# The first 60 steps of a layer, ordered by a list scheduler in the kernel instead of by hand-set pacing

## The chip, the cores and the metric

The kernel runs on one core of one Trainium2 chip. The metric is device time in microseconds (us) of one execution; the time of a kernel is the median of several runs.

## The reference

Three stages follow one another on 4 x 576 = 2304 tokens of width 512. Attention with 8 heads of 64: k and v are first averaged over groups of 8 positions (72 remain), then softmax(q k' / 8) v'. A gated layer with hidden width 1536:

```
gate = 1.0 / (1.0 + np.exp(-(x @ w_gate)))
val = x @ w_val
return (gate * val @ w_out).astype(np.float32)
```

Last, a mixture of 8 experts of width 1024 whose gates are normalised by 8 rounds of row and column division. The gated layer's weights are float64.

## The kernel before, in words

**Tiling.** The tokens are cut into 6 blocks of 384 (`NBLK`), and the 1536 hidden columns into 12 pieces of 128 (`NF1`). A step (j, f) of the gated layer takes block j and piece f: a gate product G and a value product V (12 matmuls each, L286: 4 pieces of the inner dimension times 3 passes over high and low halves), g = sigmoid(G) * V (sigmoid L1026 on ScalarE, product L1030 on VectorE), the high half of g (L1031, ScalarE) and its low half (L1034, VectorE), and an output product X of 12 matmuls (L644, `x2_step`) which sums into four PSUM banks. The table `steps1` sets the order of the 72 steps: blocks 0, 1 and 2 are interleaved over the first 36, then blocks 3, 4 and 5 follow one after the other. Steps 0 to 59 are those of blocks 0 to 4.

**Attention of a block** must end ahead of the block's first step: loads of k, v and q on SP's queue, sums over k (`pool_k`, VectorE) and over v (`pe_pool_v` on TensorE for two batches, `pool_v` on VectorE for the others), six groups of scores (`scores`), row maxima and subtraction (`less_max`), exponential (`softmax`), division (`invert`, `divide`), six groups of transposes (`turn_a`), three groups of `values`, and the split of the result into a high (L495) and a low half (L496), `xs`.

**Weights.** Each 128 x 512 piece of a weight (a chunk, 36 in all, named g, v or o) comes as float64 words into one of 4 tiles `wide`, is scaled (L197 on ScalarE, or L206 on VectorE for the first two), narrowed to float32 by five VectorE operations (L167, L168, L171, L172, L175) into one of 4 tiles `made`, and split into a high (L252) and a low half (L254) in one of 11 tiles `wa`. Its first user splits it; it is stored to DRAM (`words`), and blocks 2 to 5 load it from there. So VectorE prepares 12 chunks for the first six steps, and 24 more by step 29.

**What sets the order.** Each engine works off its own list, in the order in which the program issues. Attention is a generator (`attention`) cut by `yield` into pieces; the loop over the steps calls `slot` three times a step, and a running credit lets it take a piece there. `slot` also issues a whole chunk's narrowing when the running sums `until["dve"]` and `until["pe"]` (fixed costs added up as instructions are issued) leave room. `need` issues whatever a product still lacks, at once. Attention of block 0 and the first two score groups of block 1 are written out ahead of the first step; X of step n is issued behind G and V of step n + 1.

Of the kernel before, what the change touches and what calls it, by code (L numbers as in the profile page):

```python
# [9 lines left out]
F32 = mybir.dt.float32  # L10
# [10 lines left out]
def attention_moe_moe_kernel(  # L21
# [119 lines left out]
    n_wload = [0]  # L141
    n_split = [0]
    pools = {}
    later = []
    n_tick = [0]


    until = {"dve": 0, "pe": 0}
    loaded, scaled = [], []

    def load_wide():
        i = n_wload[0]
        if i >= n_wide:
            return
        n_wload[0] += 1
        t = xring.tile([128, KT * TB], U32, tag="fx", name="wide", bufs=NWIDE)
        nc.sync.dma_start(out=t[:, 0:1024], in_=WSRC["gvo"[i % 3]][i // 3].bitcast(U32))
        loaded.append((i, t[:, 0:1024].rearrange("p (c w) -> p c w", w=2)))

    def narrow_ops(i, raw):  # L160

        low, high = raw[:, :, 0], raw[:, :, 1]
        y = pools["at"].tile([128, 512], F32, tag="made", name="made", bufs=NMADE)
        x = y.bitcast(U32)
        v = nc.vector
        return y, [
            lambda: v.tensor_scalar(out=x, in0=high, scalar1=0x80000000, scalar2=None, op0=ALU.bitwise_and),  # L167
            lambda: v.scalar_tensor_tensor(  # L168
                out=x, in0=high, scalar=3, in1=x, op0=ALU.logical_shift_left, op1=ALU.bitwise_or
            ),  # L170
            lambda: v.tensor_scalar(out=high, in0=x, scalar1=0xFF800000, scalar2=None, op0=ALU.bitwise_and),  # L171
            lambda: v.scalar_tensor_tensor(  # L172
                out=f32(low), in0=low, scalar=2.0**-52, in1=f32(high), op0=ALU.mult, op1=ALU.mult
            ),
            lambda: v.tensor_tensor(out=y, in0=f32(low), in1=y, op=ALU.add),  # L175
        ]

    owing = [0]

    def narrow_tick():  # L180

        n_tick[0] += 1
        while owing[0]:
            owing[0] -= 1
            load_wide()
        if scaled and scaled[0][0] < n_used[0] + NMADE:
            i, raw = scaled.pop(0)
            y, ops = narrow_ops(i, raw)
            for op in ops:
                op()  # L190
            until["dve"] += 2950
            made[i] = y, n_tick[0]
            owing[0] += 1
        if loaded and not scaled:
            i, raw = loaded.pop(0)
            high = raw[:, :, 1]
            nc.scalar.activation(out=f32(high), in_=f32(high), func=AF.Copy, scale=2.0**-112)  # L197
            scaled.append((i, raw))

    def scaled_ops():  # L200

        i, raw = loaded.pop(0)
        high = f32(raw[:, :, 1])
        y, ops = narrow_ops(i, raw)
        return [
            lambda: nc.vector.tensor_scalar(  # L206
                out=high, in0=high, scalar1=2.0**-112, scalar2=None, op0=ALU.mult
            )
        ] + ops + [lambda: made.update({i: (y, -1)})]

    made = {}
    n_used = [0]
# [7 lines left out]
    stores = []  # L220
    n_kept = [0]

    def keep(k):

        while len(stores) > k:
            m, w = stores.pop(0)
            nc.sync.dma_start(out=words[m], in_=f32(w).rearrange("p s c -> p (s c)"))
            n_kept[0] += 1

    def split_chunk():  # L230

        i = n_split[0]
        if i >= len(chunks):
            return False
        m, first = source(i)
        if first:
            if m not in made or (loaded and n_tick[0] == made[m][1]):
                return False
# [1284 lines left out]
```

## Time and profile before

| what | us |
|---|---|
| median of 3 runs (2117.67 to 2124.04) | 2123.05 |
| the profiled execution's own time | 2118.32 |
| its span, first to last instruction | 2116.6 |
| TensorE busy (96%) | 2041.9 |
| VectorE busy (59%) | 1257.3 |
| ScalarE busy (36%) | 771.5 |

The profile is of one execution. An engine is busy while it executes; the time between is idle, and the profile names what ended each wait. PE is TensorE's matmuls, PEld its weight loads, DVE VectorE, ACT ScalarE, POOL GpSimd, SP the queue that issues the transfers. Busy times of matmuls overlap a little, as they are pipelined. The granted clock is 1.00 where TensorE runs at 2.4 GHz and 0.50 at 1.2 GHz; a stretch with both has a value between.

### The profile page before, as it was taken

How to read it: one execution, taken by the hardware profiler on the slowest of the kernel's cores; microseconds unless marked ns; L12 is line 12 of the kernel's file. 1: busy time of each engine (PE TensorE's matmuls, PEld its weight loads, DVE VectorE, ACT ScalarE, POOL GpSimd, SP SyncE). 2: the span in 40 equal slices, each digit the busy share in tenths (PEclk: the TensorE clock that was granted, in tenths of full speed). 3: DMA queues.
4: the chain of work that ended last, by engine and by line, in shares of the span. 5: the costliest groups of instructions: out<-in, count | busy, mean ns of one | idle time of the engine just before them, and what ended most of it. 6: DMA issues, size and time to landing. Idle time of an engine off the chain costs nothing.

```text
span 2116.6 us, 33177 instructions
## 1 busy us (share of the span) xinstructions
PE 2041.9 (96%) x12721; PEld 1943.6 (92%) x12721; DVE 1257.3 (59%) x2276; ACT 771.5 (36%) x1517; POOL 711.8 (34%) x645
## 2 busy tenths in 40 slices
PE   7778999999999999999999999999999999999998
PEld 5678989999997988998888999999999999999998
DVE  6677873523226877666665656565565556565655
ACT  4423322222224444344343444444443333333332
POOL 0000001010214474544542656655664222222322
PEclk9889999999999999999999999999999999999999
DMA  6447666776976686766768887788779876767674
GB/s 222 151 177 242 225 223 235 250 261 215 348 297 239 253 309 246 269 250 243 262 231 342 308 279 277 278 291 284 280 275 342 291 264 237 260 232 261 236 255 157
DMA packets 171853, 544.82 MB, mean 257 GB/s; under 512 B 15984, under 2 KB 65136, under 8 KB 155312
## 3 DMA queue, kind: packets, MB, share of 16 engines
q1 hardware_dynamic: 171216, 541.14, 71.8%
q8 instruction: 100, 1.64, 0.3%
q0 software_dynamic: 480, 1.57, 0.2%
q14 instruction: 57, 0.47, 0.1%
HBM read 376.72 MB, written 165.94 MB: 256 GB/s over the span
## 4 chain that ended last, share of the span: by engine, by line
PE 86%; DVE 7%; DMA 3%; ACT 3%; issue 1%; POOL 0%; SPq 0%; ACTq 0%; DVEq 0%; POOLq 0%
PE big L1263 22%; PE at L1111 18%; PE gv L1111 14%; PE big L1142 12%; PE gv L286 11%; PE big L644 5%; PE at L397 1%; PE at L485 1%; DMA wide<-in_moe_w_out_dram 1%; DVE wa L254 1%; DVE wide L172 1%; DVE made L168 1%; ACT wa L252 1%; DVE made L175 1%; DMA b<-w2d 1%
## 5 line engine op out<-in xcount | busy, mean ns | idle before, releaser
L286 PE MATMUL gv<-xs,wa 128*128 128x384 f32 x1728 | 334.1, 346 | 16.7 <-DVE g L1030 11.6
L1202 POOL TENSOR_TENSOR s<-hs,s 128x384 fp32r<-128x384 f32 x192 | 194.9, 1016 | 412.1 <-ACT s L1205 261.2
L286 PEld LDWEIGHTS gv<-xs,wa 128*128 128x128 f32 x1728 | 306.8, 193 | 24.9 <-DVE g L1030 14.1
L1142 PE MATMUL big<-w2hl,h 128*128 128x512 f32 x1152 | 297.0, 394 | 0.0
L1245 DVE SCALAR_TENSOR_TENSOR acc<-big,prob,acc 128x256 f32<-128x256 f32 (+1 forms) x462 | 254.7, 585 | 46.1 <-PE big L1263 46.1
L1142 PEld LDWEIGHTS big<-w2hl,h 128*128 128x128 f32 x1152 | 213.9, 188 | 34.3
L1111 PE MATMUL at<-xf,fs 128*128 128x384 f32 x1152 | 236.3, 340 | 3.7 <-ACT c L1314 2.7
L1111 PE MATMUL gv<-xf,fs 128*128 128x384 f32 x1152 | 233.4, 337 | 0.0
L1111 PE MATMUL at<-xf,fa 128*128 128x384 f32 x1152 | 228.0, 337 | 5.1 <-DVE gv L1332 1.8
L1111 PEld LDWEIGHTS at<-xf,fa 128*128 128x128 f32 x1152 | 198.5, 188 | 11.9 <-DVE gv L1332 2.5
L1111 PEld LDWEIGHTS at<-xf,fs 128*128 128x128 f32 x1152 | 196.8, 188 | 8.8 <-ACT c L1314 3.0
L1111 PEld LDWEIGHTS gv<-xf,fs 128*128 128x128 f32 x1152 | 198.2, 189 | 5.4 <-issue 0.2
L644 PE MATMUL big<-h,wa 128*128 128x384 f32 x864 | 166.0, 341 | 5.8 <-ACT wa L252 5.3
L1263 PE MATMUL big<-t,s 128*128 128x256 f32 x1152 | 162.7, 282 | 0.8 <-DVE acc L1245 0.8
L678 POOL TENSOR_TENSOR fx<-x,fx 128x768 fp32r<-128x768 f32 x10 | 18.4, 1836 | 426.8 <-ACT fx L677 426.8
L644 PEld LDWEIGHTS big<-h,wa 128*128 128x128 f32 x864 | 153.5, 192 | 7.8 <-ACT wa L252 6.2
L1263 PE MATMUL big<-b,a 128*128 128x256 f32 x1152 | 158.7, 283 | 2.0 <-DVE a L1192 1.9
L1263 PEld LDWEIGHTS big<-t,s 128*128 128x128 f32 x1152 | 157.1, 189 | 1.0 <-DVE acc L1245 1.0
L1263 PEld LDWEIGHTS big<-b,a 128*128 128x128 f32 x1152 | 153.5, 190 | 2.7 <-DVE a L1192 2.6
L1327 DVE TENSOR_TENSOR gv<-gv,c 128x384 f32<-128x384 f32 x64 | 36.2, 566 | 196.4 <-PE gv L1111 189.8
L1171 DVE SCALAR_TENSOR_TENSOR acc<-big,prob,acc 128x512 f32<-128x512 f32 x144 | 107.5, 747 | 70.8 <-PE big L1142 68.9
L1205 ACT ACTIVATE s<-hs 128x384 fp32r<-128x384 f32 x192 | 100.6, 524 | 110.9 <-DVE hs L1198 110.9
(184 smaller groups left out, 3067.2 us busy)
## 6 DMA issues: line engine op xcount, KB each, us to landing
wa<-words SPq DMA_DIRECT2D x144, 512.0 KB, 4.6
fs<-fsd SPq DMA_DIRECT2D x64, 1024.0 KB, 8.0
fa<-fad SPq DMA_DIRECT2D x64, 768.0 KB, 6.4
b<-w2d SPq DMA_DIRECT2D x192, 256.0 KB, 5.0
raw<-in_moe_w_dram SPq DMA_DIRECT2D x64, 512.0 KB, 7.6
fsd<-fs SPq DMA_DIRECT2D x32, 1024.0 KB, 6.2
w2d<-w2hl SPq DMA_DIRECT2D x32, 1024.0 KB, 3.9
fad<-fa SPq DMA_DIRECT2D x32, 768.0 KB, 5.8
```

The lines of the kernel that those rows point to most:

```text
L168: lambda: v.scalar_tensor_tensor(out=x, in0=high, scalar=3, in1=x, op0=ALU.logical_shift_left, op1=ALU.bitwise_or),
L172: lambda: v.scalar_tensor_tensor(out=f32(low), in0=low, scalar=2.0**-52, in1=f32(high), op0=ALU.mult, op1=ALU.mult),
L286: nc.tensor.matmul(out=out_, lhsT=a[s], rhs=b[m], start=(i == 0), stop=(i == n - 1))
L644: nc.tensor.matmul(out=x2p[d][:, :TB], lhsT=w[s][:, d * 128 : (d + 1) * 128], rhs=gs[j, f][m], start=(first and i == 0), stop=(last and i ...
L1111: nc.tensor.matmul(out=pt[:, :TB], lhsT=w[:, s, i, k], rhs=t[:, o, k], start=(start and m == 0), stop=(m == 5), skip_group_check=True,)
L1142: nc.tensor.matmul(out=py, lhsT=h[:, s, cs], rhs=w2hl[n][:, o, fh], start=(m == 0), stop=(m == 5))
L1171: nc.vector.scalar_tensor_tensor(out=acc[t], in0=py, scalar=pr, in1=acc[t], op0=ALU.mult, op1=ALU.add)
L1202: nc.gpsimd.tensor_tensor(out=t[:, 1], in0=x, in1=f32(t[:, 0]), op=ALU.subtract)
L1205: nc.scalar.activation(out=t[:, 0], in_=x, func=AF.Copy)
L1245: nc.vector.scalar_tensor_tensor(out=o, in0=src, scalar=pr, in1=o, op0=ALU.mult, op1=ALU.add)
L1263: nc.tensor.matmul(out=o, lhsT=hp[n0 + k, h][:, s, i * 128 : (i + 1) * 128], rhs=pieces2[n0, w][:, k, b], start=(first and m == 0), stop=( ...
L1327: nc.vector.tensor_tensor(out=vc, in0=vc, in1=c2, op=ALU.add)
```

## The change

The generator, `slot`, `need`, the credit and the running sums go. Each piece of the work of steps 0 to 59 becomes a task with an engine, a duration in us, the tasks that it needs, the places in tile rings that it takes and gives back (`room`, `frees`), a key (the step by which it is due, with an offset) and at times an earliest step. `Plan.run` keeps a clock for each engine. At each moment a free engine takes the task with the lowest key among those whose inputs have ended and whose room is free; taking it issues its instructions. So the lists of the engines follow the reckoned times. SP's transfers end at the reckoned end of all earlier ones plus size over 0.34 MB/us, plus 1.9 us.

Other differences: block 1's softmax is done like block 0's (one exponential with a sum for each head, straight from the scores; `j < DIRECT`); the narrowing of a chunk is two tasks (`narrow_high`, `narrow_low`) and its split two more; the division inverts for each 128 rows by itself; all of the attention of blocks 0 and 1 is due ahead of the first step. Steps 60 to 71 are issued by the loop as before.

```
+    class Plan:
+        LAG = 0.1
+        RATE = 0.34
+        REACH = 1.9
...
+        def run(self):
...
+            while left:
...
+                for e, l in queues.items():
+                    if free[e] > now:
+                        continue
+                    for t in l:
+                        if all(d.end is not None and d.end + self.LAG <= now for d in t.deps) and self.fits(t):
+                            break
+                    else:
+                        continue
+                    l.remove(t)
...
+                    t.emit()
+                    free[e] = now + t.dur
+                    t.end = now + t.dur
+                    if t.size:
+                        self.link = max(self.link, now + t.dur) + t.size / self.RATE
+                        t.end = self.link + self.REACH
...
+        def chunk(i):
...
+            n -= 0.9
+            w = add(n - 5, "SP", 0.4, lambda: load_wide(m), room=[("wide", 1)], size=0.524)
+            eng, dur = ("DVE", 0.42) if m < 2 else ("ACT", 0.68)
+            s = add(n - 0.3, eng, dur, lambda: scale_wide(m, eng), [w])
+            a = add(n, "DVE", 1.13, lambda: narrow_high(m), [s], room=[("made", 1)])
+            b = add(n, "DVE", 1.82, lambda: narrow_low(m), [a], frees=[("wide", 1)])
+            c = add(
+                n, "ACT", 0.63, lambda: split_high(i), [b], room=[("wa", 1)], cond=turn_of(i), after=took
+            )
+            d = add(n, "DVE", 0.69, lambda: split_low(m), [c], frees=[("made", 1)])
...
+        V_LATE = 0.3
+        DIRECT = 2
+        LEAD = {0: 30.0, 1: 28.0, 2: 6.0, 3: 10.0, 4: 10.0, 5: 10.0}
...
+        def attend(j):
+            n = float(at_step[j, 0] if j else 0)
+            lead = LEAD[j]
+            lo = n - lead
+            if j == 1:
+                lo, lead = -24.0, 24.0 + n - 0.5
...
+                    m = add(
+                        key, "DVE", 0.93 if j >= DIRECT else 0.6, partial(A.maxima, j, t, g), [s],
...
+                xl = add(key, "DVE", 0.69, partial(A.x_low, j, t), [xh], frees=gives(("x", j, t)), step=step)
...
+        def products(n, prev_x):
...
+            G = add(n, "PE", 2.09, product_of("g"), x_ready[j] + [ready["g", j, f], prev_g[0]], room=[("gv", 1)], frees=final("g"), after=begun)
+            SG = add(n + 0.2, "ACT", 0.49, sigmoid, [G], room=[("g", 1)], frees=[("gv", 1)])
+            V = add(
+                n + 0.3, "PE", 2.09, product_of("v"), [G, ready["v", j, f]],
...
+            MU = add(n - 1, "DVE", 0.56, times, [SG, V], frees=[("gv", 1)])
+            HH = add(n - 1, "ACT", 0.52, high, [MU], room=[("h", 1)])
+            HL = add(n - 1, "DVE", 0.57, low, [HH], frees=[("g", 1)])
...
+            X = add(
+                n + 0.9, "PE", 2.09, finish, [HL, ready["o", j, f], prev_x],
...
+        for n in range(N):
+            x = products(n, x)
+        plan.run()
```

**Where instructions move.** On SP's list at the start of the program (kr and vr are tiles of k and v, qt of q, wide of weights), before:

```order
L316 DMA kr<-in_k_dram 128x576 x2
L359 DMA qt<-in_q_dram 128x512
L316 DMA kr<-in_k_dram 128x576 x2
L359 DMA qt<-in_q_dram 128x512 x2
L157 DMA wide<-in_moe_w_gate_dram 128x1024
L330 DMA vr<-in_v_dram 128x512 x4
L330 DMA vr<-in_v_dram 64x512
L316 DMA kr<-in_k_dram 128x576 x4
L359 DMA qt<-in_q_dram 128x512
```

and now:

```order
L246 DMA kr<-in_k_dram 128x576 x4
L257 DMA vr<-in_v_dram 128x512 x4
L257 DMA vr<-in_v_dram 64x512
L261 DMA qt<-in_q_dram 128x512 x3
L246 DMA kr<-in_k_dram 128x576 x4
L257 DMA vr<-in_v_dram 128x512 x2
L261 DMA qt<-in_q_dram 128x512
L147 DMA wide<-in_moe_w_gate_dram 128x1024
L147 DMA wide<-in_moe_w_val_dram 128x1024
```

The first q stood behind two tiles of k; it now stands behind four of k and five of v, and all three q of block 0 come together.

On VectorE's list around the first products of gate and value (g<-g,gv), with the operations on `wide` and `made` that narrow a chunk, wa its split, xs the input of a block and den and e the softmax, before:

```order
L415 TENSOR_REDUCE mx<-at 128x4
L416 TENSOR_TENSOR e<-at,mx 128x288
L1030 TENSOR_TENSOR g<-g,gv 128x384
L1034 TENSOR_TENSOR h_533<-g,h_532 128x384
L167 TENSOR_SCALAR made<-wide 128x512
L168 SCALAR_TENSOR_TENSOR made<-wide,made 128x512
L171 TENSOR_SCALAR wide<-made 128x512
L172 SCALAR_TENSOR_TENSOR wide<-wide 128x512
L175 TENSOR_TENSOR made<-wide,made 128x512
L254 TENSOR_TENSOR wa<-made,wa 128x512
```

and now:

```order
L400 SCALAR_TENSOR_TENSOR xs_630<-at,xs_629 128x4x128
L162 TENSOR_SCALAR made<-wide 128x512
L163 SCALAR_TENSOR_TENSOR made<-wide,made 128x512
L200 TENSOR_TENSOR wa<-made,wa 128x512
L172 TENSOR_SCALAR wide<-made 128x512
L175 SCALAR_TENSOR_TENSOR wide<-wide 128x512
L178 TENSOR_TENSOR made<-wide,made 128x512
L1031 TENSOR_TENSOR g<-g,gv 128x384
L162 TENSOR_SCALAR made<-wide 128x512
L163 SCALAR_TENSOR_TENSOR made<-wide,made 128x512
L1038 TENSOR_TENSOR h_800<-g,h_799 128x384
L200 TENSOR_TENSOR wa<-made,wa 128x512
```

Before, the first g and its low half stood together, and a whole chunk of five operations behind them. Now the two pieces of a chunk, splits and the parts of g alternate, and the last low half of block 1's input (the first row) stands ahead of the first g.

On ScalarE's list around the first sigmoid (g<-gv behind its table load; wide<-wide scales a chunk that has landed, a<- keeps a transposed group), before:

```order
L495 ACTIVATE xs_463<-big 128x4x128
L495 ACTIVATE xs_463<-at 128x4x128
L252 ACTIVATE wa<-made 128x512
L197 ACTIVATE wide<-wide 128x512
L1026 ACT_TABLE_LOAD
L1026 ACTIVATE g<-gv 128x384
L352 COPY vp<-at 72x512
L1031 ACTIVATE h_532<-g 128x384
```

and now:

```order
L396 ACTIVATE xs_581<-big 128x4x128
L375 COPY a<-at 72x512
L153 ACTIVATE wide<-wide 128x512 x3
L396 ACTIVATE xs_629<-at 128x4x128
L196 ACTIVATE wa<-made 128x512
L1028 ACT_TABLE_LOAD
L1028 ACTIVATE g<-gv 128x384
L153 ACTIVATE wide<-wide 128x512
L1028 ACTIVATE g<-gv 128x384
L1035 ACTIVATE h_799<-g 128x384
L196 ACTIVATE wa<-made 128x512
```

Three scalings now stand in a row ahead of the last high half of block 1's input and the first sigmoid, where one stood. On TensorE's list, eight groups of scores stood ahead of the first gate product, and all twelve of blocks 0 and 1 do now; each X stood behind the G and the V of the next step, and now often stands behind its G alone.

## Rows read from the trace of the kernel before

**Rows 1.** Busy time by stretch: length, PE, PEld, DVE, ACT, POOL, clock, DMA share, GB/s.

```profile
0.00:30.00 30.00, 21.20 (x133) 14.48 (x133) 20.52 (x45) 14.44 (x61) 1.45 (x9) 1.00 0.83 289
30.00:160.30 130.30, 98.66 (x594) 86.50 (x594) 87.01 (x156) 46.47 (x78) 0.00 (x0) 0.84 0.49 159
160.30:340.00 179.70, 166.82 (x948) 160.59 (x948) 125.47 (x228) 58.44 (x105) 3.68 (x2) 0.98 0.64 219
340.00:556.70 216.70, 215.72 (x1379) 202.68 (x1377) 78.06 (x138) 58.87 (x101) 23.87 (x13) 1.00 0.76 257
556.70:2116.00 1559.30, 1539.55 (x9674) 1479.34 (x9673) 946.21 (x1711) 593.33 (x1174) 682.83 (x621) 1.00 0.75 270
```

**Rows 2.** Waits of PE, 0 to 160.3 us: total us, times, longest us.

```profile
PE at L470 <- DVE e L455: 10.5, 2, 10.1
PE big L397 <- DMA qt<-in_q_dram: 6.0, 1, 6.0
PE at L470 <- ACT a L472: 5.7, 4, 2.6
PE big L644 <- ACT wa L252: 5.3, 1, 5.3
```

**Rows 3.** Waits of PE, 160.3 to 556.7 us.

```profile
PE gv L286 <- DVE g L1030: 11.6, 7, 3.7
```

**Rows 4.** Timeline of PE: start us, length us, line, operation, tiles, idle before.

```profile
139.62 0.60 PE L470 MATMUL at<-ident,e 128*72 128x128 f32 x4
...
146.68 1.09 PE L485 MATMUL at<-a,vp 72*64 72x128 f32 x16
...
151.99 2.24 PE L644 MATMUL big<-h,wa 128*128 128x384 f32 x12
...
158.23 2.24 PE L644 MATMUL big<-h,wa 128*128 128x384 f32 x12
160.31 4.33 PE L286 MATMUL gv<-xs,wa 128*128 128x384 f32 x24
...
176.12 1.11 PE L397 MATMUL at<-kp,qt 64*128 64x72 f32 x8
177.15 2.35 PE L286 MATMUL gv<-xs,wa 128*128 128x384 f32 x12
...
556.71 4.32 PE L286 MATMUL gv<-xs,wa 128*128 128x384 f32 x24
```

**Rows 5.** Timeline of DVE, same columns.

```profile
11.49 0.46 DVE L418 TENSOR_REDUCE mx<-big 128x4 f32<-128x288 f32 x1
11.98 0.17 DVE L419 TENSOR_SCALAR mx<-mx 128x4 f32<-128x4 f32 x1
...
17.49 2.73 DVE L368 TENSOR_REDUCE kp<-kr 128x72 f32<-128x576 f32 x4
20.13 0.16 DVE L450 TENSOR_SCALAR den<-den 128x8 f32<-128x8 f32 x1
...
20.57 0.76 DVE L455 TENSOR_TENSOR e<-e,den 128x576 f32<-128x576 f32 x1
...
84.29 0.56 DVE L1030 TENSOR_TENSOR g<-g,gv 128x384 f32<-128x384 f32 x1 [3.19 <-PE gv L286]
85.43 0.56 DVE L1034 TENSOR_TENSOR h<-g,h 128x384 fp32r<-128x384 f32 x1 [0.59 <-ACT h L1031]
...
88.23 0.42 DVE L167 TENSOR_SCALAR made<-wide 128x512 uint32<-128x512 uint32 x1
...
90.60 0.69 DVE L175 TENSOR_TENSOR made<-wide,made 128x512 f32<-128x512 f32 x1
```

**Rows 6.** Busy time in the opening, 9.2 to 31.7 us, columns as in group 1.

```profile
9.20:31.70 22.50, 20.44 (x140) 14.02 (x139) 18.68 (x43) 14.63 (x62) 0.00 (x0) 1.00 0.78 278
```

**Rows 7.** Transfers into the tiles `wide`, 0 to 160 us, issue to landing.

```profile
DMA to landing us min/median/max: 6.5/7.7/11.9
```

**Rows 8.** Wait of ACT for weight loads, 0 to 160.3 us.

```profile
ACT wide L197 <- DMA wide<-in_moe_w_gate_dram: 3.3, 1, 3.3
```

More of the change, by code (lines that the diff above doesn't have):

```diff
@@ L160, in narrow_ops @@
-    def narrow_ops(i, raw):
-        low, high = raw[:, :, 0], raw[:, :, 1]
[L163 to L198, printed above, removed]
@@ L381, in pieces @@
+        def pieces(self, j, t):
             c = j * TB + t * 128
@@ L983, in attention_moe_moe_kernel @@
[L983 to L996 removed]
+        N = at_step[NBLK - 1, 0]
@@ new lines, in with_bank, with emit, gives, turn_of @@
+        def with_bank(key, f):
+            def emit():
+                tag = tag_of[key] = free_tag()
+                used[tag] += 1
+                f((tag, plan.limits[tag]))
+            return emit
+        def gives(key):
+            return [(lambda: tag_of.pop(key), 1)]
+        next_chunk = [0]
+        def turn_of(i):
+            return lambda: next_chunk[0] == i
+        def took():
+            next_chunk[0] += 1
+        ready = {}
+        stored = {}
+        high_of = {}
+        OFF = {"g": 0.0, "v": 0.3, "o": 1.0}
@@ new lines, in attention_moe_moe_kernel, with gate_words @@
+        visited = set()
+        prev_g = [None]
+        for j in range(2):
+            attend(j)
+        for i in range(3):
+            chunk(i)
+        done_chunks = 3
+        done_att = 2
+        x = None
+        def gate_words():
+            nc.sync.dma_start(out=wg_raw, in_=moe2_w_gate.rearrange("(k p) e -> p k e", p=128))
+        gw = add(5, "SP", 0.4, gate_words, size=0.02, step=4)
+        gw = add(9, "ACT", 0.25, lambda: nc.scalar.activation(out=wg_hi, in_=wg_raw, func=AF.Copy), [gw], step=6)
@@ new lines, in attention_moe_moe_kernel @@
+        add(9, "DVE", 0.25, lambda: nc.vector.tensor_sub(out=wg_lo, in0=wg_raw, in1=f32(wg_hi)), [gw], step=6)
+        for i in range(3, len(chunks)):
+            if at_step[chunks[i][1:]] < N + 3:
+                chunk(i)
+        for j in range(2, NBLK):
+            attend(j)
+        for n in range(N):
+            x = products(n, x)
+        plan.run()
+        at_pool.__exit__(None, None, None)
+        pools["late"] = ctx.enter_context(tc.tile_pool(name="late", bufs=1, reuse_waits="tile"))
```

836 lines of the change are left out of this document (433 added, 403 removed).

## The prediction

> **What bounds the kernel now.** I read the busy time by stretch first, then what TensorE waited for, then the two timelines, since a share over the whole span says nothing of the opening. By stretch [rows 1], from 556.7 us on TensorE is busy 98 to 99% at full clock and the change does not reach there; from 340 to 556.7 it is busy 215.72 of 216.70. All that can be won lies before 340 us: TensorE is idle 8.8 us of the first 30, 31.6 us of the next 130.3 and 12.9 us of the next 179.7. In the second stretch the granted clock is also 0.84, that is, about a third of it was at 1.2 GHz and not 2.4. The waits [rows 2] name no single culprit: 10.5 us for a division on VectorE, 6.0 for the first q, 5.7 and 5.3 for copies on ScalarE. Behind them is VectorE, busy 87.01 of 130.3 us there [rows 1], with the pieces in an order that makes others wait. After 160.3 us, 11.6 us in seven waits are for g, the product gate times value, that stands in VectorE's queue behind weight preparation [rows 3].
>
> Two marks on TensorE's timeline serve as milestones [rows 4]. The first gate product of block 2 (the ninth step, G8) starts at 160.31 us. The gate product of the 62nd step (G61), just past the part that the scheduler issues, starts at 556.71. Ahead of either mark both kernels have nearly the same work behind them, so the change is worth what G61 moves. The step from the start of one output product to the next is 158.23 - 151.99 = 6.24 us, or 2.08 for each of its three products, with no wait.
>
> **Opening, up to the first gate product G0.** The change moves both attention blocks 0 and 1 ahead of G0 and drops that product's old place. SP now issues four k tiles and five v transfers ahead of the first q, where two k tiles stood ahead of it: two k tiles (0.59 MB) and v (1.18 MB) more, 1.77 MB at the 289 GB/s of the first 30 us [rows 1], 6.1 us. The first q came when TensorE's wait for it ended, at 6.0 [rows 2]; now at about 12, and the first row maximum is taken at about 13. What TensorE does meanwhile (the sums over v) is not on the path.
>
> VectorE then has, up to the low half of x that G0 needs last [rows 5]: 12 row maxima at 0.46 + 0.17, 7.6 us; four sums over k of block 1, 2.7; six divisions, each 20.13 to 21.33, 7.2; five low halves of x, 3.5; three weight chunks narrowed, each 88.23 to 91.29 or 3.06, and the first two operations (1.1) of a fourth, 10.3; two splits and the low halves at the 0.69 of the last narrowing operation, of the same width, 1.4 for the splits; two scalings at the 0.42 of the first one, 0.8. The sum is 33.5, so G0 at 46.6 if VectorE never waits. In the like stretch it was busy 18.68 us of 22.5 and waited 3.8 [rows 6]. It now has two blocks to change between; I take 2.5 us and **G0 at 49**. The other engines end earlier: ScalarE was busy 14.44 us for one block in the first 30 us, so some 29 for two; TensorE 21.20, and some 42 with both, at most.
>
> **From G0 to G8.** TensorE has eight steps, 49.9 us, and block 2's attention: six score groups at 1.11, six transpose groups at 0.60 and three value groups at 1.09, 13.5 us; and 0.11 us each of some eight times that a product follows attention (2.35 long, not 2.24) [rows 4], 0.9 us. That is 64 us. VectorE is as full: nine chunks less those first two operations, 26.4, and ten splits, 6.9; g and its low half of six steps at 0.56 each, 6.7 [rows 5]; six maxima with subtraction of block 2, two operations of 0.46, 5.5; the low half of x left, 0.7; some 46 us until the twelfth chunk is ready, against 50 us until TensorE asks for it. Then 18 us of divisions, sums, g and x lead to block 2's input; so **65 us** by VectorE too, and any wait of it shows.
>
> Three things that no row shows are bounded and added. (1) Clock: at worst the whole stretch at 1.2 GHz doubles 24 products, +50; at best nothing. The stretch with two holes of over 5 us got 0.84; with holes of 1 to 3 us I take a few short drops, +4. (2) Weight loads that land later than the scheduler reckons. It reckons 0.4 us to issue, 0.52 MB at 0.34 MB/us and 1.9, 3.8 us in all; the loads took 6.5 at least and 7.7 in the median [rows 7]. Eight chunks are loaded into freed tiles on the way to G8, so 0 to 8 x 3.9 = 31 us. Near 0 is right for VectorE: a load is issued when its tile is free, three chunks (3 x 3.75 = 11.2 us) ahead of its use. But ScalarE gets the scaling of that chunk in its list where the load should have landed, and all behind it waits; I take +5. The Trainium skill, DMA: Bandwidth & Descriptors, section "Anatomy of one DMA — SWDGE (gpsimd) path", gives about 2.0 us and bytes / 436e9, so an estimate of 3.2 us here and +0 for this term. By it the sum below would be 2066; but these loads are on SP's queue, and the trace has twice that time. (3) VectorE's own waits on TensorE and ScalarE in this stretch: at worst the share of the opening, 3.8 of 22.5, which is 11 us, at best nothing; (2) holds most of them, so I add none.
>
> So G8 comes at 49 + 65 + 4 + 5 = 123, **37 us earlier** than 160.3.
>
> **From G8 to G61.** Before, 396.4 us with 13.9 us of idle TensorE [rows 1] and two drops of the clock after waits, some 3 us by the 0.98 granted. VectorE has 24 chunks left, 24 x 3.75 = 90 us, in the 130 us until the last is used: it runs ahead, and g can come first, since a chunk is now two pieces (1.1 and 1.9) and not one of 3.06. Against that the output product X now often stands right behind one gate product, where it stood behind a gate and a value product. From g to the end of its low half is 84.29 to 85.99, 1.70 us [rows 5], and one product is 2.08: 0.38 us to spare. I leave 7 of the 17 us and take **10 us**. Block 1's softmax with one exponential by head costs ScalarE a few us and spares VectorE the subtraction; both lie ahead of G0 and are counted there. Separate inversions for each 128 rows add four small operations of about 0.2 us a block on VectorE, hidden by its lead. Weight words reloaded for blocks 2 to 4 are the same transfers; TensorE was full there and I expect it full.
>
> Sum: 37 + 10 = 47 us off the profiled execution of 2118.3 us: 2071. That execution lies 4.7 us below the median of the runs, near their lowest; with a little of that the forecast is **2072 us**.
>
> **Rivals.**
> *Late loads hold ScalarE.* If the scalings up to G8 each wait the full difference, term (2) is 31 and not 5: 26 us less, **2098**. For it: scalings now stand three in a row ahead of the last high half of x and the first sigmoid; before, ScalarE took them one at a time with 3.3 us of waiting [rows 8]. Against it: only waits that end last count, and each round starts later by what the last slipped.
> *The clock eats it.* TensorE stays at 1.2 GHz from G0 to G8: +50 in place of +4, **2118, no change**. For it: small attention matmuls now fill the time ahead of G0. Against it: the first 30 us had the same small matmuls and were granted 1.00 [rows 1].
> *A rigid order.* The lists are fixed by reckoned times and the engines keep to them. If X meets an uninterrupted 1.9 us piece on VectorE ahead of g in every step, TensorE loses about 0.95 us on average (half the piece) in each of 59 steps, 56 us, which turns the gain of 47 into a loss: **2127, slower**. It decides from 0.9 us a step on. For it: only 0.38 us to spare. Against it: VectorE was busy 70% between 160 and 340 us [rows 1] and 36% after, so such meetings are too few, and the reckoned durations (0.69 for a low half, 0.57 for g's) are those of the rows or longer.
> *The change does less than it says*, the order in the first 160 us coming out much as before, is excluded by the order of instructions: 12 score groups, not eight, now stand ahead of G0.
>
> **How the numbers follow.** Forecast with its own range of 2055 to 2088, 70%; late loads, 2088 to 2105, 14%; better than 2055, 4%; the clock and no change, 5%; the rigid order, 7%. The best case is VectorE never waiting, terms (1) and (2) at nothing and the later stretch clean: 47 + 2.5 + 4 + 5 + 7 = 65 us, 2053; the range takes it in and ends above with the late loads, 2053 to 2100. About 0.3% (6 us) is what a measurement of this kernel can tell from no change: a fifth of the no-change case falls below that, so faster 0.89, same 0.04, slower 0.07.
>
> **What would show it.** Right: G0 near 49, G8 near 123, G61 near 510; TensorE's idle before 340 us near 30 us and most of it ahead of G0; the waits for g after G8 down from 11.6 us. The 10.1 us wait for a division gone. Term (2): waits of ScalarE for weight loads before G8, well above 3.3 us, with TensorE idle beside them. Wrong: TensorE waiting 0.9 us or more at each X; a granted clock below 0.7 between G0 and G8; or new idle time of TensorE between 340 and 556 us.

## The result, and the profile after

| | before | changed |
|---|---|---|
| median of 4 runs, us | 2120.36 | 2082.82 |
| lowest to highest, us | 2115.99 to 2124.04 | 2081.35 to 2086.78 |
| profiled execution, us (its span) | 2118.3 (2116.6) | 2083.54 (2081.8) |
| ratio changed / before | | 0.9827, 95% interval 0.98 to 0.9853 |

The kernel is 1.7% faster, inside the range and 11 us above the forecast. Busy time of the changed kernel by stretch, columns as in [rows 1], which it answers; its stretches are cut at the starts of G8 and G61:

```profile
0.00:30.00 30.00, 20.50 (x78) 11.74 (x78) 13.34 (x33) 10.32 (x56) 1.45 (x9) 0.85 0.82 280
30.00:121.20 91.20, 87.69 (x624) 76.78 (x623) 81.09 (x164) 54.16 (x129) 0.00 (x0) 0.96 0.62 220
121.20:340.00 218.80, 212.29 (x1233) 203.79 (x1234) 151.53 (x273) 72.94 (x128) 14.91 (x8) 0.98 0.69 236
340.00:524.20 184.20, 176.61 (x1117) 165.05 (x1116) 66.44 (x116) 47.44 (x81) 15.11 (x8) 0.99 0.75 252
524.20:2081.00 1556.80, 1540.27 (x9675) 1481.45 (x9673) 946.60 (x1711) 592.63 (x1173) 681.17 (x620) 1.00 0.74 269
```

From 30 us to G8 TensorE is idle 3.5 us, where [rows 1] has 31.6 us between 30 and 160.3. The last line, past the scheduler's part, is as before. But from 340 to 524.2 it is idle 7.6 us, and before it was idle 1.0 of a longer stretch. The milestones, on the timeline of TensorE (they answer [rows 4]):

```profile
8.71 5.37 PE L287 MATMUL at<-vr,spread 128*72 128x512 f32 x6 [8.71 <-DMA vr<-in_v_dram]
14.01 1.14 PE L309 MATMUL at<-kp,qt 64*128 64x72 f32 x8
...
20.85 1.93 PE L287 MATMUL big<-vr,spread 128*72 128x512 f32 x2
...
54.57 1.66 PE L226 MATMUL gv<-xs,wa 128*128 128x384 f32 x8
...
121.20 0.45 PE L226 MATMUL gv<-xs,wa 128*128 128x384 f32 x1 [0.69 <-ACT xs L396]
...
524.27 1.89 PE L226 MATMUL gv<-xs,wa 128*128 128x384 f32 x10
```

G0 at 54.57, G8 at 121.20, G61 at 524.27. One correction is needed before they are compared. The row that the forecast took for G8 of the kernel before, 160.31 [rows 4], is G9. The product that starts at 154.07 is G8:

```profile
154.07 2.24 PE L286 MATMUL gv<-xs,wa 128*128 128x384 f32 x12
```

The X that stands between the two in [rows 4], at 158.23, is that of step 7, since this kernel issues X of a step behind G and V of the next. A count settles it: from 160.31 to 556.71 there are 1248 gate and value instructions, 24 a step, which is 52 steps and ends at G61 only if it begins with G9. So the gain up to G8 is 154.07 - 121.20 = 32.9 us; from G8 to G61 it went from 402.6 to 403.1 us, no gain at all (between the sigmoids of the two steps, 402.6 and 400.5); and the rest is 2.4 us shorter, no more than this part differs between kernels that have it alike (see e1). At G61 both kernels have issued the same 3048 instructions on TensorE. At G8 the changed one has issued one X more (700 against 688), 2.1 us of work: for like work it gains 35.0 us up to there and loses 2.5 behind.

The gain up to G8 is mostly idle time of TensorE, 40.4 us before and 13.0 now. The rest is pace, 5.4 us less busy time for more instructions:

```profile
0.00:154.07 154.07, 113.63 (x689) 94.75 (x689) 102.04 (x194) 60.41 (x137) 1.45 (x9) 0.87 0.54 183
0.00:121.20 121.20, 108.19 (x700) 88.52 (x700) 94.43 (x196) 64.48 (x183) 1.45 (x9) 0.93 0.67 235
```

What TensorE waited for in the changed kernel between G8 and G61 (total us, times, longest us):

```profile
PE big L509 <- ACT h L1035: 4.9, 4, 1.7
PE big L509 <- DVE h L1038: 4.7, 7, 1.2
```

The waits for g [rows 3] are gone. In their place the output product X waits 9.6 us in eleven waits for the two halves of h, the split of g that it reads. To see where, the stretch is cut at the sigmoids of steps 8, 32 and 61, here of the kernel before (length, busy TensorE, clock, DMA share, GB/s):

```profile
156.41:335.62 179.21, 166.33 (x946) 0.98 0.64 218
335.62:559.04 223.42, 222.44 (x1418) 1.00 0.77 259
```

and here of the changed kernel:

```profile
126.03:281.66 155.63, 155.63 (x902) 1.00 0.68 235
281.66:526.55 244.89, 231.79 (x1450) 0.99 0.75 251
```

Between steps 8 and 32 the changed kernel has no idle time whatever. It issues 44 instructions fewer there, 12 of which (one X) it did ahead of step 8; the other 32 it leaves for later. From step 32 on it is idle 13.1 us, where the kernel before was idle 1.0. The gain of one half is lost in the other. One of the eleven waits, on the timeline of the changed kernel:

```profile
499.42 2.35 PE L226 MATMUL gv<-xs,wa 128*128 128x384 f32 x12
499.75 0.85 ACT L548 ACTIVATE fx<-tt 128x768 fp32r<-128x768 f32 x1
500.49 0.51 ACT L1035 ACTIVATE h<-g 128x384 fp32r<-128x384 f32 x1
500.67 1.83 POOL L549 TENSOR_TENSOR fx<-tt,fx 128x768 fp32r<-128x768 f32 x1 [21.30 <-ACT fx L548]
...
501.03 1.88 DVE L1038 TENSOR_TENSOR h<-g,h 128x384 fp32r<-128x384 f32 x1 [1.65 <-ACT h L1035]
...
502.97 0.44 PE L509 MATMUL big<-h,wa 128*128 128x384 f32 x1 [1.02 <-DVE h L1038]
```

g was ready at 499.38. ScalarE, though, first ends a copy of a transposed group that had begun at 499.26, then copies `fx`, a piece of `after_block` (the gate logits and pair sums that follow a block's last step; a gate piece from here on), and begins the high half at 500.49, 1.1 us after g. VectorE's low half runs beside GpSimd's subtraction of the same piece and takes 1.88 us, not 0.56. X has one product's time (2.1 us) of cover and waits. To the plan these pieces are tasks on TensorE (`next(gate, None)`), of 0.05 us each, 2.2 for the one with products: the copies, subtractions and sums that they issue on three other engines have no duration and no due time there.

### The profile page after: what moved, and what is told of

Same layout as the page of the kernel before. It is cut to its first block, busy times and chain, and to the rows that moved or that the text cites. A ratio compares the mean times of both kernels' runs of the same rounds, so it can differ in the third digit from the quotient of the medians.

```text
span 2081.8 us, 33236 instructions
## 1 busy us (share of the span) xinstructions
PE 2037.4 (98%) x12721; PEld 1938.8 (93%) x12721; DVE 1259.0 (60%) x2293; ACT 777.5 (37%) x1562; POOL 712.7 (34%) x645
## 4 chain that ended last, share of the span: by engine, by line
PE 92%; DVE 3%; DMA 2%; ACT 1%; issue 1%; POOL 0%; SPq 0%; ACTq 0%; DVEq 0%; POOLq 0%
PE big L1371 22%; PE at L1219 19%; PE gv L1219 14%; PE gv L226 13%; PE big L1250 13%; PE big L509 7%; PE at L309 1%; DMA vr<-in_v_dram 1%; DMA fa<-fad 1%; PE at L384 1%; DVE h L1038 0%; DMA b<-w2d 0%; PE at L370 0%; PE at L226 0%; PE big L287 0%
## 5 line engine op out<-in xcount | busy, mean ns | idle before, releaser
L226 PE MATMUL gv<-xs,wa 128*128 128x384 f32 x1728 | 322.3, 339 | 2.7 <-DVE xs L400 1.0
L226 PEld LDWEIGHTS gv<-xs,wa 128*128 128x128 f32 x1728 | 301.3, 189 | 7.1 <-issue 1.5
```

What stands on the lines that cost most here:

```text
L226: nc.tensor.matmul(out=out_, lhsT=a[s], rhs=b[m], start=(i == 0), stop=(i == n - 1))
```

## The experiments

The later stretch: **theory A** says that the gate pieces, unknown to the plan, stand in the way of h; **theory B** that X's place behind one product is enough by itself; **theory D** that nothing is to be had there, and a wait taken away only moves. The opening: **theory C** says that v ahead of q costs 5 us; **E** that another chain sets G0; **F** that TensorE's clock decides; **G** that the half pace (1.2 GHz, at which like instructions take nearly twice as long) comes whatever precedes it; **J** that idle time brings it on; **H** and **I** are on block 1's place and form. ScalarE's sigmoid of a step stands for the milestones (its start, us; in the last column the end of the span):

| kernel | step 0 | step 8 | step 32 | step 61 | span |
|---|---|---|---|---|---|
| before | 33.66 | 156.41 | 335.62 | 559.04 | 2116.6 |
| changed | 58.77 | 126.03 | 281.66 | 526.55 | 2081.8 |
| e1 X behind V | 58.40 | 126.32 | 283.33 | 519.06 | 2078.4 |
| e2 gate after low half | 58.09 | 125.33 | 281.00 | 515.53 | 2072.5 |
| e3 fx on VectorE | 57.78 | 125.09 | 280.65 | 522.74 | 2077.5 |
| e4 q first | 63.18 | 126.83 | 282.05 | 527.57 | 2083.8 |
| e5 e4 + idle products | 54.84 | 118.52 | 273.74 | 519.35 | 2077.0 |
| e6 e2 + idle products | 56.76 | 123.90 | 279.67 | 514.21 | 2073.1 |
| e7 block 1 late | 38.22 | 135.62 | 290.78 | 533.45 | 2091.1 |
| e8 block 1, one softmax | 57.17 | 127.41 | 282.63 | 525.88 | 2082.5 |
| e9 e2 + e5 | 64.00 | 127.66 | 282.88 | 518.22 | 2077.5 |
| e10 e9 + early q | 63.92 | 128.45 | 283.67 | 518.19 | 2076.7 |
| e11 e6 + early q | 56.69 | 123.86 | 279.58 | 514.35 | 2071.4 |
| e12 e11 + gap filled | 53.11 | 119.19 | 274.41 | 510.89 | 2068.3 |

**e1.** In `products`, X of a step also depends on V of the next.

```diff
+            if x_of:
+                x_of.pop().deps.append(V)
...
+            x_of.append(X)
```

> One edit: the output product X of step n is made to depend on the value product V of step n+1 as well, so that two products (4.2 us) stand between the last input of the halves of h and the product that reads them, instead of one (2.1 us). The changed kernel as it is: 2082.8 us; between step 9 and step 61 TensorE waits 9.6 us for the halves of h in 11 waits. Theory A (the gate pieces, which the plan knows as 0.05 us of TensorE, put 0.83 us copies, 0.96 us subtractions and a GpSimd operation in the way of h, and X stands too near to bear it): the 11 waits vanish, 6 to 9 us come back, 2074 to 2077 us. Theory B (X's place behind one gate product is at fault by itself, whatever stands in the way): the same here; the next two runs part them. Rival theory D (the later stretch has nothing to give: a wait that is taken away only moves, or comes back as a lower granted clock): the waits for h vanish and others, for g, for a split weight or for a free bank, take their place, 2081 to 2085 us.

2081.24 us (2075.43 to 2082.53), ratio to before 0.9811 (0.9791 to 0.9831). All eleven waits for h went, and step 61 came 7.5 us earlier. In their place, between G8 and G61:

```profile
PE at L226 <- POOL fx L549: 2.2, 2, 1.5
PE at L309 <- DMA qt<-in_q_dram: 2.1, 2, 1.6
PE at L226 <- ACT fx L548: 1.4, 1, 1.4
```

Of the 7.5 us the medians show 1.6, and the intervals overlap with those of the changed kernel. In the profiled execution the stretch from step 61 to the end is 1559.3 us against 1555.3, with the same instructions on TensorE; over all the kernels here it lies between 1554.8 and 1559.3, and where 4 us of it come from is open. The run doesn't tell A from B.

**e2.** A gate piece is released only behind the low half of the step that it is planned in.

```diff
+            for t in gates_at.pop(n, ()):
+                t.deps.append(HL)
...
+                    gates_at.setdefault(n + 1 + k, []).append(t)
```

> One edit: a gate piece that follows a block's last step is released only behind the low half of h of the step in which it is planned, so that ScalarE's copies of the gate stand behind the high half instead of ahead of it. Theory A: the waits of X for ScalarE's half (4.9 us in 4) fall to under 1.5 us; those for VectorE's half (4.7 us in 7) fall only where the copy had delayed the low half; 2078 to 2081 us. Theory B: waits of X unchanged within 1.5 us in sum, 2082 to 2084 us. Theory D: the waits fall, the time stays, 2081 to 2084 us.

2076.46 us (2074.2 to 2078.02), ratio 0.9793 (0.9776 to 0.981): more than any theory gave. X stands behind one product as before, and its waits are not down but gone. TensorE's waits of 1 us or more in all between G8 and G61 (lt holds the gate logits):

```profile
PE at L309 <- DMA qt<-in_q_dram: 3.3, 1, 3.3
PE gv L226 <- DVE g L1031: 1.8, 1, 1.8
PE at L586 <- DVE lt L577: 1.5, 2, 0.7
PE gv L226 <- DVE xs L400: 1.0, 1, 1.0
```

The busy time by stretch, for the two windows of steps 8 to 32 and 32 to 61:

```profile
125.33:281.00 155.67, 155.67 (x902) 1.00 0.67 236
281.00:515.53 234.53, 227.74 (x1450) 0.99 0.74 260
```

The second is 10.4 us shorter than in the changed kernel: 6.3 us of it idle time, and 4.1 us less busy time for the same 1450 instructions. The latter is what a wait can cost beyond itself: in the changed kernel the X that had waited 1.74 us at 330.11 took 3.80 us, the next one that had waited (338.99) 2.77, and of the one after that (348.08) eleven of the twelve instructions 3.71, instead of 2.2 for all; the granted clock was 0.75 from 332 to 338 and from 350 to 354. B falls: X's place is harmless once the gate pieces stand behind h. A holds, and with e1 it takes both, a gate piece ahead of h and an X that stands near.

**e3.** The gate pieces' subtractions go from GpSimd to VectorE.

```diff
-        eng = nc.vector if j == NBLK - 1 else nc.gpsimd
+        eng = nc.vector
```

(and likewise in the four pair sums)

> One edit: the subtractions of the gate pieces that run on GpSimd (1.84 us each) go to VectorE. It isolates what GpSimd does to VectorE beside it. Theory A: the long low halves (1.88 to 2.16 us instead of 0.56) are all gone, the longest row of that line is under 0.7 us between step 9 and step 61; X's waits for VectorE's half fall from 4.7 us to under 2 us; VectorE gets 0.6 to 1.0 us more per subtraction, which can delay g once or twice; 2079 to 2083 us. Theory B: the long low halves have another cause and stay; the waits stay; 2082 to 2085 us.

2081.61 us (2079.18 to 2084.19), ratio 0.982 (0.9803 to 0.9837). The low halves and, for comparison, g's product between G8 and G61 (mean ns of one behind the busy time):

```profile
L1038 DVE TENSOR_TENSOR h<-g,h 128x384 fp32r<-128x384 f32 x52 | 28.8, 554 | 10.4 <-ACT h L1035 10.4
L1031 DVE TENSOR_TENSOR g<-g,gv 128x384 f32<-128x384 f32 x52 | 28.7, 552 | 58.8 <-PE gv L226 54.9 <-ACT fx L548 3.6
```

and the same two lines of the changed kernel:

```profile
L1038 DVE TENSOR_TENSOR h<-g,h 128x384 fp32r<-128x384 f32 x52 | 34.3, 660 | 14.6 <-ACT h L1035 14.6
L1031 DVE TENSOR_TENSOR g<-g,gv 128x384 f32<-128x384 f32 x52 | 28.7, 551 | 66.1 <-PE gv L226 62.4 <-ACT fx L548 3.6
```

The long low halves are gone; so GpSimd made them. (In e2, where GpSimd's work stands behind the low half, all 52 take 0.543 to 0.560 us as well.) Only the waits for VectorE's half fell, to 1.4 us; those for ScalarE's rose from 4.9 to 6.2. Steps 32 to 61 take 242.1 us, 2.8 less; the median is 1.2 us lower, within the spread of the runs. Against e2's 10.4 us that is about a quarter, with the subtractions now on VectorE's account; the waits that are left are those behind ScalarE's copies.

**e4.** v's lateness in the plan from 0.3 to 3.0, so that q is loaded ahead of it.

```diff
-        V_LATE = 0.3
+        V_LATE = 3.0
```

> One edit: the lateness number of v's load is raised from 0.3 to 3.0, so that SyncE issues the first block's q ahead of v, and TensorE's list has the scores ahead of the six matmuls that spread v. Theory C (about 5 us of the opening go to v: TensorE waits 8.7 us for v's transfer and its matmuls fill 8.7 to 14.0 before the first score): the first score starts at 8.7 to 10 instead of 14.0, G0 at 49 to 51 instead of 54.6, and the time falls by 3.5 to 5.5 us to 2077.5 to 2079.5. Rival E (another chain sets G0: the wide words and the splits, or the maxima on VectorE): the scores start 4 to 5 us earlier and G0 moves by less than 1.5 us; 2081.5 to 2083.5 us.

2085.04 us (2083.77 to 2085.83), ratio 0.9834 (0.9817 to 0.9851). Neither C nor E. The first score started at 7.88 us, 6.1 earlier, yet the sigmoid of step 0 came 4.4 us later. TensorE's timeline, early and late in the opening:

```profile
13.93 1.98 PE L309 MATMUL big<-kp,qt 64*128 64x72 f32 x8
15.84 1.98 PE L287 MATMUL at<-vr,spread 128*72 128x512 f32 x2
...
43.59 1.11 PE L309 MATMUL big<-kp,qt 64*128 64x72 f32 x8
44.63 1.08 PE L287 MATMUL big<-vr,spread 128*72 128x512 f32 x2
```

The same eight scores take 1.98 us and then 1.11, the same pair of spread products 1.98 and then 1.08. The half pace holds from the first score to about 42: eight transposes at 38.37 still take 1.91 us, and eight at 51.03 take 1.04. The granted clock of this trace's opening reads 1.00 throughout, so here only the durations tell it. In the changed kernel it shows in both from 20.9 to 34.6 (the pair at 20.85 takes 1.93; granted clock 0.50) and again from 41.4 to 44.8; with the 5.3 us of the six spread products at 8.71 that is some 22 us, not 34. G0 comes at 57.91, 3.3 us later. The other 1.1 us at the sigmoid is ScalarE's: the scaling ahead of it waited 2.2 us for its load.

**e5.** e4, and nine products without use (128x384, on ones, into a bank that nothing reads) ahead of the first score.

```diff
+        warm = base.tile([128, TB], F32, tag="g", name="g", bufs=2)
+        nc.vector.memset(warm, 1.0)
+        pw = bank("gv", 2)
+        for i in range(9):
+            nc.tensor.matmul(out=pw[:, :TB], lhsT=warm[:, :128], rhs=warm, start=(i == 0), stop=(i == 8))
```

> The order with q ahead of v of the run before, and nine matmuls without use (128x384, on a tile of ones, into a bank that nothing reads) ahead of TensorE's first score. In the run before the first score started at 7.9 us instead of 14.0, but from 12.05 to 37.5 the spread matmuls took 1.98 us for two and the scores 1.98 us for eight, against 1.08 and 1.11 later, and step 0's sigmoid came at 63.2 instead of 58.8. Theory F (TensorE's half pace in that stretch took the gain; how busy it was before it decides): the nine matmuls bring the full pace from the first score on, and it holds: sigmoid of step 0 at 49 to 54, 2075 to 2081 us. Rival G (the pace falls again as soon as the scores and short gaps come, whatever ran before them): pairs of spread matmuls at 1.9 to 2.0 us somewhere between 14 and 37, sigmoid of step 0 at 58 to 64, 2082 to 2087 us.

2080.73 us, ratio 0.9824 (0.9795 to 0.9853), with runs from 2071.57 to 2087.56, so not told apart from the changed kernel. On TensorE the nine products are 18 instructions. In the profiled execution the full pace held until 31 us; the half pace came at 32.25 instead of 12.05, and step 0's sigmoid 8.3 us earlier than in e4. e9 has the same opening, and there the half pace set in at 13.25:

```profile
1.53 8.46 PE L803 MATMUL gv<-g 128*128 128x384 f32 x18 [1.53 <-DVE g L800]
...
13.25 1.95 PE L287 MATMUL at<-vr,spread 128*72 128x512 f32 x2 [1.20 <-issue]
```

and here it did not, at the same place:

```profile
1.53 7.49 PE L803 MATMUL gv<-g 128*128 128x384 f32 x18 [1.53 <-DVE g L800]
...
12.28 1.05 PE L287 MATMUL at<-vr,spread 128*72 128x512 f32 x2 [1.20 <-issue]
```

Both follow the same 1.2 us of idle time. But the two executions differ ahead of it: the same 18 instructions take 0.97 us more in e9, so the full pace came later there, by an estimate of some 2 us (twice the difference, as like instructions take nearly twice as long at half pace). One order of work, then, and G0 at 51.29 and at 58.55: the pace of this opening is not settled by the order. (The sigmoids of step 0 lie 9.2 us apart; the 1.9 us more are ScalarE's, which in e9 waited 2.4 us for a load ahead of it and here 0.8.) F holds for what the clock costs, but the full pace did not last; G holds for its wandering.

**e6.** The same nine products in e2, ahead of the first spread product (same diff).

> The kernel with the gate pieces behind the low half (2076.5 us) with the same nine matmuls without use ahead of the first spread matmul of v, in the 8 us in which TensorE waits for v's transfer. Theory F: the first six spread matmuls (5.4 us in the changed kernel) take about 3.2 us, and the half pace between 20.9 and 33 does not come back; step 0's sigmoid at 49 to 55 instead of 58.1, 2068 to 2074 us. Rival G: the six are shorter, the half pace comes at another time for as long, step 0's sigmoid at 56 to 60, 2074 to 2079 us.

2074.16 us (2073.19 to 2074.77), ratio 0.9791 (0.9771 to 0.981). The six spread products take 2.74 us instead of 5.37, the half pace comes 2 us earlier and lasts as long, step 0 gains 1.3 us: G, at the good end.

**e7.** Block 1's attention due beside step 0 instead of ahead of it.

```diff
-                lo, lead = -24.0, 24.0 + n - 0.5
+                lo, lead = 0.0, n - 0.5
```

> One edit to the changed kernel: the attention of block 1 gets the due times 0.0 to 0.5 instead of -24 to 0.5, so that it stands behind step 0's products instead of ahead of them, beside the products as in the kernel before. Theory H (the gain up to step 8 comes from the two attentions of the opening standing together ahead of step 0, as the forecast's first step has it): G0 comes 12 to 18 us earlier, step 1 waits for block 1's normalising and for its values as in the kernel before, the sigmoid of step 8 at 131 to 140 instead of 126.0, 2087 to 2097 us. Rival I (the opening is full on TensorE and the order in it does not matter; the gain comes from the finer pieces and deadlines): the sigmoid of step 8 within 3 us of 126.0, 2080 to 2086 us.

2093.5 us (2091.55 to 2097.19), ratio 0.9885 (0.9864 to 0.9906). The sigmoid of step 0 comes 20.6 us earlier, that of step 8 9.6 us later. Between 54 and 72 us TensorE is idle 3 us at a granted clock of 0.59:

```profile
54.00:72.00 18.00, 14.99 (x101) 0.59 0.65 234
```

Putting both attentions ahead of G0 is worth 10.7 us of the gain, by the medians. Of the 9.6 us at step 8, 4.3 are idle time of TensorE and 5.3 are pace: 117.35 us busy up to there, and 112.02 in the changed kernel, for the same work. H has its numbers, but for G0, which came 18.7 us earlier and not 12 to 18. But of the 30.4 us that the change gains up to the sigmoid of step 8, 20.8 are still there in e7: they come from what else the scheduler does (the finer pieces, the order by due times), which no run takes apart.

**e8.** Block 1's softmax in the form of the later blocks.

```diff
-        DIRECT = 2
+        DIRECT = 1
...
-            if j >= 2:
+            if j >= 1:
```

> One edit to the changed kernel: block 1's softmax goes back to the form of the later blocks (maxima and subtractions on VectorE, one exponential over the block on ScalarE, sums on VectorE) from the pieces per tile and head group. Theory H: the turns of block 1 start only after its last score and one long exponential; TensorE gets idle time of 4 to 10 us ahead of step 0, the sigmoid of step 0 at 62 to 69 instead of 58.8, 2085 to 2092 us. Rival I: the other work covers it, the sigmoid of step 0 or at least of step 8 within 2 us of the changed kernel's (58.8 and 126.0), 2081 to 2085 us.

2084.81 us (2084.22 to 2085.55), ratio 0.9842 (0.9822 to 0.9861). TensorE waits 3.2 us for a division, step 0 is not later, step 8 is 1.4 us later: I. The new form is worth 2 us by the medians, within the spread of the changed kernel's runs.

**e9, e10.** The edits of e2, e4 and e5 together; and with q of the blocks from the third on four steps earlier.

```diff
+                early = 4 if j >= 2 else 0
-                qt = add(at_key(0.0) - 2 + 0.1 * t, ..., step=step)
+                qt = add(at_key(0.0) - 2 - early + 0.1 * t, ..., step=step - early)
```

> The three edits together: gate pieces behind the low half, q ahead of v, nine matmuls without use ahead of the first score. If they act in separate stretches (the opening: sigmoid of step 8 at 118.5 instead of 126.0; steps 32 to 61: 234.5 us instead of 244.9), the sigmoid of step 61 comes at 508 to 510 and the time is 2064 to 2069 us. Theory D (what is taken away comes back elsewhere): 2073 to 2077 us, no better than either kernel it is made from. Rival G (the half pace wanders from run to run, as the spread of 16 us in the runs of the warmed q-first kernel may say): a median of 2066 to 2074 us with runs 8 us or more apart.

> The same, and q of the blocks from the third on is loaded 4 steps earlier, since with the gate pieces behind the low half TensorE waited 3.35 us for one of them at 342.67. If that wait was on the path: it goes, nothing else changes, 2 to 4 us less than the run beside it. Theory D: another transfer of the same queue (a split weight, k, v) is late in its place, within 1.5 us of the run beside it.

2078.2 us (2073.53 to 2079.82), ratio 0.9805 (0.9785 to 0.9824), and 2078.29 us (2068.0 to 2080.28), ratio 0.9797 (0.9772 to 0.9823). None of the three ranges holds for e9, whose median lies above all of them. The gain of e2 in steps 32 to 61 is there in both (235.3 and 234.5 us); the opening of e5 is not. The early q changed nothing: in e9 the wait that it aims at was 0.2 us, and theory D fits.

**e11.** e6 with the early q, v ahead of q.

> Gate pieces behind the low half, nine matmuls without use ahead of the first spread matmul of v (v ahead of q, as in the changed kernel), and q of the blocks from the third on loaded 4 steps earlier. Without the last of these: 2074.2 us, with one wait of 4.0 us for such a q between step 32 and 61. If that wait was on the path: it goes and the time is 2070 to 2072.5 us. Theory D: another transfer is late in its place, 2073 to 2076 us.

2072.84 us (2071.62 to 2075.26), ratio 0.9778 (0.976 to 0.9796). The wait of 4.0 us for q went. New ones stand in its place, and step 61 did not move (514.35 against 514.21): D.

```profile
PE at L226 <- ACT fx L548: 2.4, 1, 2.4
PE at L226 <- POOL fx L549: 1.4, 1, 1.4
PE big L509 <- ACT h L1041: 1.2, 1, 1.2
```

**e12.** e11, and two more products without use where TensorE was idle for 0.8 us.

```diff
+            if (j, t, g) == (0, 1, 1):
+                for i in range(2):
+                    nc.tensor.matmul(out=pw[:, :TB], lhsT=warm[:, :128], rhs=warm, start=(i == 0), stop=(i == 1))
```

> The kernel beside it, and two more matmuls without use (0.8 us at full pace) behind the fourth group of scores, where TensorE stands idle for 0.8 us just ahead of the stretch of half pace (17.0 to 17.8, half pace from about 19 to 30). Theory J (that idle time brings the half pace on): no matmul of the opening at 1.9 to 2.0 us per pair, the sigmoid of step 0 at 50 to 53 instead of 56.8, 4 to 6 us less than the run beside it. Rival G (the scores and turns bring it, gap or no gap): the half pace comes within a few us of where it was, the sigmoid of step 0 at 55 to 60, within 2 us of the run beside it.

2071.23 us (2069.32 to 2071.37), ratio 0.9767 (0.9749 to 0.9784), the fastest here. The two products are four instructions of 1.56 us in all, not 0.8. The half pace that e11 has from 18.8 to 32 did not come; it came at 33.40, behind a wait of 0.65 us, and lasted 7 us:

```profile
18.79 1.11 PE L309 MATMUL at<-kp,qt 64*128 64x72 f32 x8
19.83 1.08 PE L287 MATMUL big<-vr,spread 128*72 128x512 f32 x2
...
32.36 1.11 PE L309 MATMUL at<-kp,qt 64*128 64x72 f32 x8 [0.65 <-ACT e L345]
33.40 1.94 PE L388 MATMUL big<-a,vp 72*64 72x128 f32 x16
```

Step 0 gained 3.6 us, which is nearer to J, though J had asked for no half pace at all; the median gained 1.6, which is within G's 2 us. And the two executions differ ahead of the gap as well (the 18 instructions take 8.35 us here and 7.91 in e11), as e5 and e9 do, which part behind the same idle time. So J is not shown, and what decides on the pace stays open.

## Why the prediction was right, and where it was not

**The sum.** 47 us were forecast off the profiled execution, and 34.8 came. The parts: up to G8 32.9 and not 37; from G8 to G61 none and not 10; behind it 2.4 that were not forecast and that the spread of this part covers. (The best case, 2053, lies just outside the stated 2055 to 2088, though the text has it inside.)

**G0 at 49: late, 54.57.** The step that failed is "The other engines end earlier", with TensorE at "some 42 with both, at most", and "What TensorE does meanwhile (the sums over v) is not on the path". VectorE's work was no more than forecast (30.2 us busy from its first row maximum at 15.19 on, forecast 33.5), but TensorE set G0. It could not begin until v landed at 8.71, and then was busy 43.44 us of the 45.8 left; even the forecast's 42 us from there on end at 50.7. What made its work so long is the pace: some 22 us of it at half pace (see e4), which costs about 11 us by an estimate, the half of it, and no term of the sum stood for it. In e12, with v first as here and half pace from 33.5 to 40.3 only, G0 came at 48.90. The place of v does not decide it: e4 takes v out of the way, and G0 comes later.

The half pace could have been read in the kernel before. Its granted clock shows 1.00 there [rows 1] [rows 6], but like instructions take nearly twice as long up to some 20 us:

```profile
15.76 1.06 PE L470 MATMUL at<-ident,e 128*72 128x128 f32 x4
16.62 3.61 PE L340 MATMUL big<-vr,spread 128*72 128x512 f32 x4
...
21.91 0.60 PE L470 MATMUL big<-ident,e 128*72 128x128 f32 x4
22.35 2.88 PE L340 MATMUL big<-vr,spread 128*72 128x512 f32 x6
```

So "the first 30 us had the same small matmuls and were granted 1.00", the forecast's case against its rival of the clock, does not hold, and of the 21.20 us of TensorE that it doubled some 12.6, those of the first 20 us, were work at half pace.

**G0 to G8 in 74 us: early, 66.6.** The 65 us of work was right. The additions weren't needed. (1) The clock: granted 1.00 from 54.5 to 121.2; the half pace lies ahead of G0. (2) Late loads: ScalarE waited 2.9 and 1.1 us for them in five waits, and TensorE shows no wait that ends on one. They landed 6.2 us after issue in the median, and at best 3.3, where [rows 7] has 7.7 and 6.5. Term (1) was sized by rows of a stretch with long holes, term (2) by transfers that stood in another order. The two errors, +5.6 at G0 and -7.4 behind it, hid one another; that G8 at 123 came out close is luck.

**37 us earlier at G8.** The new time was right to 2 us, the old one was read a step too late (160.31 is G9, G8 is 154.07). For like work the gain is 35.0. One product more or less cannot be seen in a row of the timeline; counting instructions to the next milestone shows it.

**10 us from G8 to G61.** "I leave 7 of the 17 us" failed. That g would come first was right: its waits [rows 3] are gone, and up to step 32 TensorE never stops. The cover of 0.38 us was named, and its danger looked for on VectorE, in weight preparation. What came in between were the gate pieces: ScalarE's copies of 0.85 us ahead of the high half, and GpSimd beside the low half. They are in the code as `next(gate, None)`, 0.05 us on TensorE; the forecast gave them nothing, much as the plan did. With them behind the low half (e2) this stretch takes 390.2 us between the sigmoids of steps 8 and 61, against 402.6 before: the 10 us were there to be had, and the kernel came to 2076.5 us.

**The rivals.** Late loads cost little, and the clock did not fall between G0 and G8; it cost its time ahead of G0. The rigid order came true in small: not 0.95 us in each of 59 steps but 9.6 us in eleven waits, behind gate pieces and not weight preparation. The change did what it says, and e7 shows what its opening is worth. TensorE's idle time before 340 us is 19.5 us, of the 30 that were forecast. "New idle time of TensorE between 340 and 556 us" was named as a sign of error, and it came: 7.6 us.

## What to carry to other kernels

A list scheduler is only as good as what its tasks admit to issuing. Go through every task that calls into other code, and give each instruction that this code puts on another engine a duration and a due time, or tie the task behind the last urgent piece of its step; here that was worth 6.4 us by the medians (e2), where loading q ahead of v (e4) gained nothing. When milestones are compared across two orders of work, count instructions to a common point, and compare busy with idle time in each half of a stretch: a total that has not moved can be a gain and a loss.

## What the runs showed of the hardware

VectorE's subtraction of two tiles takes 0.56 us alone and 1.88 us where GpSimd's subtraction runs beside it: it ends at 502.91, and GpSimd at 502.50. With GpSimd's work moved (e3) all 52 average 0.554 us. VectorE's product of g, with one operand in PSUM, averages 0.551 in the changed kernel and 0.552 in e3; the three that ran beside GpSimd in the changed kernel (at 273.35, 298.37 and 425.23) took 0.553 to 0.555. Order counts too: a low half that began at 275.15, 0.13 us ahead of GpSimd's subtraction, took 0.55. The Trainium skill, SBUF — State Buffer, section "Who interferes with whom", says that a VectorE instruction with two SBUF inputs contends with a GpSimd instruction that reads SBUF, and that one with at most one SBUF input does not, outside the modes in which it uses both ports; the rows of g and of its low half agree. One input alone is no safeguard, though: a tensor_scalar of 128x8 elements with one SBUF input (the first step of the division, 0.16 us at 20.13 in [rows 5]) ran beside that same subtraction from 275.61 and took 1.81 us. That would fit such a mode, but no run here shows the mode.

TensorE at half pace can go unseen in the granted clock. It reads 1.00 over the opening of e4, in which like instructions take 1.98 and 1.11 us; over the first 20 us of the kernel before, with transposes at 1.06 and then 0.60; and over the changed kernel's six spread products, which take 5.37 us there and 2.74 in e6. In these traces the first reading of the clock comes only behind such a stretch (at 42, 20 and 14 us), so the 1.00 ahead of it may stand for no reading at all; that is not shown. Two executions of one and the same opening differed by 7.3 us at G0 by their pace, so a time of it from a single trace is worth little.
